# Batch 0's odd products ahead of the table scaling, and a third memset ahead of a sign change

## The chip, the cores and the metric

The kernel runs on one core of a Trainium2 chip. The metric is device time of one execution in microseconds (us); lower is better. A core has five engines that run side by side, each through its own list of instructions in order: PE (matrix products), ACT (activation and copies), DVE (vector arithmetic), POOL (a second vector engine, which also issues DMAs) and SP (which here only issues DMAs). They meet through semaphores: an instruction can be made to wait until another engine's counter has reached a value.

## The reference, cut to what matters

The input `x` is 8 sequences of 3136 positions by 256 features. The first block mixes it with a two-dimensional Fourier transform and keeps the real part; the second is a gated convolution with 1024 hidden features.

```python
X = np.fft.fft(x, axis=1)
X = np.fft.fft(X, axis=2)
x = X.real                               # (8, 3136, 256)

h = np.maximum(x @ w_in, 0.0)            # (8, 3136, 1024)
conv_out = sum over k of conv_w[k] * (h shifted by k - 1 along the sequence)
gate = 1.0 / (1.0 + np.exp(-conv_out))
out = h * gate @ w_out                   # (8, 3136, 256)
```

## The kernel before, in words

**The transform.** The kernel folds the sequence by its symmetries on DVE, multiplies the folded data with sine and cosine tables on PE, and combines the products on DVE into two tiles for each batch, `pt` and `qt`. The tables are `tab2` (even frequencies, `tabs[0]`) and `tab4` (odd ones, `tabs[1]`). Only half of each even table is loaded; `mirror_even(q)` (L269, ACT) writes the other half of fold class q from another class, with a sign. `mend_row(0, half)` (L310, ACT) multiplies the last rows of class 3 of `tab2`, for cosine and sine at once, with 1 or 0.5: it *halves the weight* of one row. It is one instruction on 2 partitions and 786 elements.

**Units.** The products of a batch come in units. A unit has products on PE (`part(0)` and `part(1)` issue the first two of them and the rest), a `copy` on ACT of one half of the PSUM result, and a `fin` on DVE. Of the four odd units of batch 0, `odds[0]` and `odds[2]` are `odd_even` units, which read `tab4`; `odds[1]` and `odds[3]` are `odd` units, whose part 1 is four products each that read class 2 of `tab2` and four weight tiles that `scaled()` (L217, ACT) has written into tiles named `h`. The copies are L394 and L417, the `fin` functions L398 to L430. After the odd units comes the *feature* unit, whose eight small products (into `pd`) read `tab2`, classes 3, 2, 1 and 0; then even units. In the profile these products are at L93, which is a helper that all products go through, so they are told apart by tile names.

**The waits.** The order on each engine is the order in which the code issues instructions. The waits are worked out from tiles: a read waits for the writes before it in code order, a write waits for the reads before it. `mend_row(0)` writes one instruction's worth of cosine and sine rows. Seen as one stretch of memory it runs from class 3 of the cosine table to class 3 of the sine table, and the sine table's class 2 lies inside. The products of `odds[1]` and `odds[3]` that read the sine table's class 2 therefore count as touching what `mend_row(0)` writes, though no element is shared.

**The steps.** After the transform of batch 0, the second block runs in *steps*, one for each batch, chunk of the sequence and slice of 128 hidden features. A step t has: `products` into `pb` and `pa` (PE), `copies` of `pb` into `nb` (L840, ACT), `combine` (L848, DVE, two instructions that add and clamp into the step's tile `h`), `seed` (L819, ACT), `first_tap` (L854, ACT), `middle` (L858, a DMA issued by POOL that adds `h` into `g`), `last_tap` (L863, DVE), `sigmoid` (L882, ACT), `gate` (L890, DVE) and `mm2` (the products into `po`, PE). `mm2` comes five cycles behind `products`. `row_of(step)` allots a step's tile `h` and, in a sequence's first chunk, has POOL zero its two edge columns (L825, a memset); `combine` waits for that.

**Around the first steps.** Up to about 104 us DVE also turns weights into f32 (`exponent` L651, `power` L655 on ACT, `sign` L661, `mantissa` L664, `lower` L667, `value` L670). `flip()` copies a row of `qt` by DMA into `er`; `store()` lets POOL change the sign of half of it (L490, the *sign change*), and SP then writes it out (L491).

The lines that the change moves on POOL are these, in the step loop's cycle t:

```python
        if 1 <= t < n - 1:
            row_of(steps[t + 1])
        if t < n:
            middle(steps[t])
        run("pool")          # cycle 0: store()
```

Of the kernel before, what the change touches and what calls it, by code (L numbers as in the profile page):

```python
# [37 lines left out]
def kernel(  # L38
# [226 lines left out]
    def mirror_even(q):  # L265

        for st, s in enumerate(((1.0, 1.0), (-1.0, 1.0), (-1.0, -1.0), (1.0, -1.0))[q]):
            of = st if q % 2 else 1 - st
            act(tabs[0][0:KR, st, q, HM:HE][:, ::-1], tabs[0][0:KR, of, q, 0:HE - HM], AF.Copy, scale=s)  # L269
# [37 lines left out]
    def mend_row(par, half):  # L307

        row = tabs[0][96:NP, 0:2, HQ - 1] if par == 0 else tabs[1][96:NP, 0:2, 1]
        act(row, row, AF.Copy, scale=half[96:NP])  # L310
# [401 lines left out]
    half = const.tile([P, 1], F32, name="half")  # L712
# [101 lines left out]
    def seed(s):  # L814

        b, c, f = s
        ch, n, fs = cut(s)
        pa[s] = psa.tile([P, 512], F32, name="pa", tag="pa")
        act(pa[s][:, 0:n], eb[b, c], AF.Copy, scale=ge[:, f:f + 1])  # L819

    def row_of(s):
        hs[s] = hp.tile([P, HW], F32, name="h", tag="h")
        w = chunks[s[1]].w
        if chunks[s[1]].zeros:
            nc.gpsimd.memset(hs[s][:, 0:w:w - 1], 0.0)  # L825

    def products(s):
        b, c, f = s
        ch, n, fs = cut(s)
        pb[s] = psb.tile([P, 512], F32, name="pb", tag="pb")  # L830
        mm(pb[s][:, 0:n], G[0:P - 1, 1, fs], PQ[b][1][0:P - 1, ch.k0:ch.k1], True, True)
        mm(pa[s][:, 0:n], G[:, 0, fs], PQ[b][0][:, ch.k0:ch.k1], False, True)

    def copies(s):

        ch, n, fs = cut(s)
        p = pb.pop(s)
        nb[s] = nbp.tile([P, 2, HN], F32, name="nb", tag="nb")
        for i, cols in enumerate((ch.fcols, ch.cols)):
            act(nb[s][:, i, cols], p[:, cols], AF.Copy, scale=-1.0 if i else 1.0)  # L840

    def combine(s):

        ch, n, fs = cut(s)
        a, c = pa.pop(s), nb.pop(s)
        h = hs[s]
        for i, (to, cols) in enumerate(((h[:, ch.front], ch.fcols), (h[:, ch.back][:, ::-1], ch.cols))):
            nc.vector._custom_dve(TENSOR_ADD_SAT, out=to, in0=a[:, cols], in1=c[:, i, cols],  # L848
                                  s0=BIG, s1=0.0)

    def first_tap(s):
        n = chunks[s[1]].w - 2
        gs[s] = gp.tile([P, HW - 2], F32, name="g", tag="g")[:, 0:n]
        act(gs[s], hs[s][:, 0:n], AF.Copy, scale=cw[:, 0, s[2]:s[2] + 1])  # L854

    def middle(s):
        n = gs[s].shape[1]
        nc.gpsimd.dma_start(out=gs[s], in_=hs[s][:, 1:1 + n], accum_op=ALU.add)  # L858

    def last_tap(s):  # L860
        g, h, f, k = gs[s], hs[s], s[2], 2
        n = g.shape[1]
        stt(out=g, in0=h[:, k:k + n], scalar=cw[:, k, f:f + 1], in1=g, op0=ALU.mult, op1=ALU.add)  # L863
# [14 lines left out]
    def sigmoid(s):  # L878

        v, p, r = shares(s)  # L880
        for c in [slice(0, r.stop)] if whole(s) else (slice(p.start, r.stop), v):
            act(gs[s][:, c], gs[s][:, c], AF.Sigmoid, scale=cw[:, 1, s[2]:s[2] + 1])  # L882

    def gate(s):

        b, c, f = s
        g, h = gs[s], hs.pop(s)[:, 1:]
        v, p, r = shares(s)
        if whole(s):
            vt(g, g, h[:, 0:r.stop], op=ALU.mult)  # L890
            return
        p = slice(p.start, r.stop)
        gt(g[:, p], g[:, p], h[:, p], op=ALU.mult)
        vt(g[:, v], g[:, v], h[:, v], op=ALU.mult)

    def keep(s):

        b, c, f = s
        r = shares(s)[2]
        if r.start < r.stop:  # L900
            nc.scalar.copy(out=left[:, f, b % 2 * LEFT:(b % 2 + 1) * LEFT], in_=gs[s][:, r])

    def mm2(s):
        b, c, f = s
        ch = chunks[c]
        tiles = [(gs[s][:, o:o + m], [(0, b, r, m)]) for o, r, m in ch.tiles]
        if ch.last and b % 2:
            tiles.append((left[:, f], [(i * LEFT, b - 1 + i, ch.rest[1], LEFT) for i in range(2)]))
        for i, (w, to) in enumerate(tiles):
            if f == 0 and i % 2 == 0:  # L910
                po[b, c, i // 2] = pso.tile([P, 2, D], F32, name="po", tag="po")
            pt = po[b, c, i // 2]
            mm(pt[:, i % 2, :], w, wout[:, f, :], f == 0 and i % 2 == 0, f == NF - 1)
            if f == NF - 1 and (i % 2 or i == len(tiles) - 1):
                del po[b, c, i // 2]
                osb = osp.tile([P, 2, D], F32, name="os", tag="os")
                for j in range(i - i % 2, i + 1):
                    nc.scalar.copy(out=osb[:, j % 2], in_=pt[:, j % 2])  # L918
                if i % 2:
                    r0, r1 = (tiles[j][1][0][2] for j in (i - 1, i))  # L920
                    nc.sync.dma_start(out=bass.AP(
                        tensor=out.tensor, offset=out.offset + (b * S + r0) * D,
                        ap=[[D, P], [(r1 - r0) * D, 2], [1, D]]), in_=osb)
                else:
                    for j, (p0, b_, r, m) in enumerate(tiles[i][1]):
                        (nc.scalar if j and s == steps[-1] else nc.sync).dma_start(out=rows[b_ * S + r:b_ * S + r + m, :], in_=osb[p0:p0 + m, 0])
        gs.pop(s)
# [11 lines left out]
    odds = [us[j] for j in (0, 1, 5, 6)]  # L939
# [28 lines left out]
        u.part(0)  # L968
    for u in odds[::2]:
        u.part(1)  # L970
    odds[0].copy()
    odds[0].fin()
    mend_row(0, half)
    odds[1].part(1)
    odds[1].copy()
    odds[1].fin()
    mirror_even(1)
    odds[2].copy()
    odds[2].fin()
    mirror_even(3)  # L980
    odds[3].part(1)
    odds[3].copy()
    odds[3].fin()
    exponent()
    mantissa()

    n = chunks[0].k1
# [14 lines left out]
            lower()  # L1002
    steps = [(b, c, f) for b in range(B) for c in range(len(chunks)) for f in range(NF)]
    per = len(chunks) * NF
    for i in range(2):
        row_of(steps[i])
    side = {}
    taken = set()
# [45 lines left out]
    for b in range(1, B):  # L1054
# [4 lines left out]
        n = per * b - (2 if b == 1 else 3) - c0  # L1059
# [12 lines left out]
    for b in range(1, B):  # L1072
        ops, singles, pres = fold_ops(b)
        c0, n = ends[b - 1], ends[b] - ends[b - 1]
# [4 lines left out]
        else:  # L1079
            if b == 2:  # L1080
                c0, n = c0 + 3, n - 3
# [16 lines left out]
    n = len(steps)  # L1098
# [6 lines left out]
    for t in range(n + LAG):  # L1105
        def run(where):
            for fn in side.get((t, where), []):
                fn()
        if 0 <= t - 4 < n:
            sigmoid(steps[t - 4])  # L1110
        if t + 1 < n:
            products(steps[t + 1])
            copies(steps[t + 1])
        run("first")
        run("act")
        if t >= LAG:
            keep(steps[t - LAG])
        if t < n:
            combine(steps[t])
        if t + 2 < n:  # L1120
            seed(steps[t + 2])
        if t < n:
            first_tap(steps[t])

        run("dve")
        if 0 <= t - 3 < n:
            last_tap(steps[t - 3])
        if 0 <= t - 4 < n:
            gate(steps[t - 4])
        if 1 <= t < n - 1:  # L1130
            row_of(steps[t + 1])
        if t < n:
            middle(steps[t])
        run("pool")
        run("load")
        if t >= LAG:
            mm2(steps[t - LAG])
        run("pe")
# [66 lines left out]
```

## Time and profile before

| what | value |
|---|---|
| device time, median of 3 runs | 1159.29 us (1159.04 to 1159.99) |
| the profiled execution: its time | 1159.72 us |
| the profiled execution: its span, first to last instruction | 1157.9 us |
| PE busy | 1137.4 us |
| DVE busy | 960.3 us |
| ACT busy | 901.4 us |
| POOL busy | 376.3 us |

Times in the profile are us from the start of the span; the mean duration of one instruction of a group is in ns. A row of the timeline is: start, duration, engine, line, operation, output tile <- input tiles, partitions x elements, count; in square brackets stands the engine's idle time before it and what ended that. Rows of like instructions that follow each other are merged. PE runs each f32 product as two records, so "x12" is six products. A letter q behind an engine's name is its queue, which issues DMAs.

### The profile page before, as it was taken

The numbers are of one execution on the slowest core, as the hardware profiler recorded it, in microseconds if no ns is written. First come the engines' busy times: TensorE is split into PE (matmuls) and PEld (weight loads), VectorE is DVE, ScalarE is ACT, GpSimd is POOL, SyncE is SP. The second block draws the span as 40 slices with busy tenths as digits, with TensorE's granted clock in tenths as the row PEclk, the third lists the DMA queues.
The fourth block names the chain that finished last, engine by engine and source line by source line (L and its number), as shares of the span: only waits on it lengthen the run. The fifth ranks groups of instructions, "written<-read, shape, count | busy, mean of one in ns | idle before, by whom it ended". The sixth has DMA issues, their size and how long they took to land.

```text
span 1157.9 us, 15068 instructions
## 1 busy us (share of the span) xinstructions
PE 1137.4 (98%) x4824; PEld 887.7 (77%) x4824; DVE 960.3 (83%) x1452; ACT 901.4 (78%) x1707; POOL 376.3 (32%) x484
## 2 busy tenths in 40 slices
PE   6999999999999999999999999999999999999998
PEld 4667787788777777778777777777778777777777
DVE  8899899988988989798878878888886767877775
ACT  3788868877787778787878778887877777888884
POOL 6425523642343242425132332422212222222223
PEclk9999999999999999999999999999999999999999
DMA  9787975876767586756676666765664656666664
GB/s 246 172 118 167 180 168 117 182 166 143 172 127 162 118 192 153 166 119 151 139 173 133 152 142 123 175 129 119 138 132 90 128 117 137 139 132 128 123 118 101
DMA packets 107595, 167.49 MB, mean 145 GB/s; under 512 B 32104, under 2 KB 62838, under 8 KB 107517
## 3 DMA queue, kind: packets, MB, share of 16 engines
q0 software_dynamic: 42160, 115.87, 51.9%
q1 hardware_dynamic: 64616, 50.53, 15.9%
q8 instruction: 38, 0.62, 0.2%
q10 hardware_dynamic: 741, 0.14, 0.1%
q14 instruction: 40, 0.33, 0.1%
HBM read 37.80 MB, written 25.74 MB: 55 GB/s over the span
## 4 chain that ended last, share of the span: by engine, by line
PE 85%; DVE 5%; ACT 5%; issue 2%; POOL 2%; DMA 1%; SPq 0%; ACTq 0%; POOLq 0%; DVEq 0%
PE po L93 53%; PE pb L93 13%; PE pa L93 13%; PE pd L93 6%; DVE g L863 1%; DVE g L890 1%; ACT os L918 1%; ACT nb L840 1%; POOL xh L129 1%; DMA xh<-in_x_dram 1%; DVE h L848 1%; ACT pa L819 1%; ACT g L882 0%; ACT g L854 0%; DMA tab<-dft_seq_dram 0%
## 5 line engine op out<-in xcount | busy, mean ns | idle before, releaser
L93 PE MATMUL po<-wout,g 128*128 128x256 f32 x3072 | 706.4, 379 | 3.8 <-DVE g L890 3.7
L93 PEld LDWEIGHTS po<-wout,g 128*128 128x128 f32 x3072 | 580.5, 190 | 149.0 <-DVE g L890 18.2
L858 POOL DMA_DIRECT2D g<-h x256 | 220.0, 859 | 729.3 <-ACT g L854 459.9
L840 ACT ACTIVATE nb<-pb 128x386 f32<-128x386 f32 (+3 forms) x512 | 227.5, 499 | 168.0 <-PE pb L93 167.1
L848 DVE CUSTOM_DVE_ANT_0 h<-pa,nb 128x386 f32<-128x386 f32 (+3 forms) x512 | 265.2, 559 | 34.8 <-PE pa L93 22.6
L882 ACT ACTIVATE g<-g,cw 128x770 f32<-128x770 f32 (+3 forms) x264 | 246.0, 935 | 46.3 <-DVE g L863 44.9
L863 DVE SCALAR_TENSOR_TENSOR g<-h,cw,g 128x770 f32<-128x770 f32 (+1 forms) x256 | 265.6, 1038 | 0.3 <-DMA g<-h 0.3
L890 DVE TENSOR_TENSOR g<-g,h 128x770 f32<-128x770 f32 (+1 forms) x248 | 240.3, 969 | 22.3 <-ACT g L882 22.1
L854 ACT ACTIVATE g<-h,cw 128x770 f32<-128x770 f32 (+1 forms) x256 | 244.1, 953 | 0.0
L93 PE MATMUL pb<-qt,G 127*128 127x387 f32 (+2 forms) x512 | 213.7, 498 | 1.5 <-ACT nb L840 1.1
L93 PE MATMUL pa<-pt,G 128*128 128x387 f32 (+2 forms) x512 | 212.1, 495 | 0.8 <-ACT pa L819 0.7
L819 ACT ACTIVATE pa<-eb,ge 128x387 f32<-128x387 f32 (+2 forms) x256 | 155.3, 607 | 2.1 <-DVE h L848 0.3
L93 PEld LDWEIGHTS pa<-pt,G 128*128 128x128 f32 x512 | 96.6, 189 | 75.6 <-issue 18.5
L129 POOL DMA_INDIRECT xh<-in_x_dram,idx x64 | 98.4, 1538 | 20.2 <-issue 12.7
L93 PE MATMUL pd<-tab,w 98*128 98x197 f32 (+2 forms) x448 | 97.6, 317 | 0.0
L93 PEld LDWEIGHTS pb<-qt,G 127*128 127x128 f32 x512 | 90.9, 190 | 8.5 <-ACT nb L840 2.9
L93 PEld LDWEIGHTS pd<-tab,w 98*128 98x128 f32 (+1 forms) x448 | 82.0, 191 | 8.9
L918 ACT COPY os<-po 128x256 f32<-128x256 f32 x196 | 57.4, 393 | 6.3 <-PE po L93 6.3
L398 DVE TENSOR_TENSOR as<-as,pd 128x196 f32<-128x196 f32 x14 | 5.0, 358 | 46.0 <-ACT as L394 46.0
L176 POOL COPY w<-xh 98x4 f32<-98x4 f32 (+1 forms) x30 | 37.5, 1251 | 7.9 <-DVE xh L170 7.9
L154 DVE TENSOR_TENSOR xh<-xh 98x1020 f32<-98x1020 f32 (+1 forms) x32 | 38.7, 1211 | 0.5 <-DMA xh<-in_x_dram,idx 0.5
L165 DVE TENSOR_TENSOR xh<-xh 98x1024 f32<-98x1024 f32 (+1 forms) x32 | 38.9, 1216 | 0.1
(150 smaller groups left out, 430.9 us busy)
## 6 DMA issues: line engine op xcount, KB each, us to landing
g<-h POOLq DMA_DIRECT2D x192, 385.0 KB, 3.9
g<-h POOLq DMA_DIRECT2D x64, 416.0 KB, 4.3
out_dram<-os SPq DMA_DIRECT2D x96, 256.0 KB
xh<-in_x_dram SPq DMA_DIRECT2D x16, 784.0 KB
eb<-ed SPq DMA_DIRECT2D x16, 193.5 KB
raw<-in_moe_w_in_dram SPq DMA_DIRECT2D x4, 512.0 KB
raw<-in_moe_w_out_dram SPq DMA_DIRECT2D x1, 2048.0 KB
eb<-ed SPq DMA_DIRECT2D x8, 209.0 KB
```

The source lines that it names most:

```text
L93: nc.tensor.matmul(o, l, r, start=start, stop=stop, skip_group_check=True)
L129: nc.gpsimd.indirect_dma_start(out=xh[b, h][0:NP, 7 - m].rearrange("p q d -> p (q d)"), out_offset=None, in_=bass.AP(tensor=x.tensor, offs ...
L165: vt(flat(to, to + 2), flat(0, 2), flat(2, 4), op=op)
L819: act(pa[s][:, 0:n], eb[b, c], AF.Copy, scale=ge[:, f:f + 1])
L840: act(nb[s][:, i, cols], p[:, cols], AF.Copy, scale=-1.0 if i else 1.0)
L848: nc.vector._custom_dve(TENSOR_ADD_SAT, out=to, in0=a[:, cols], in1=c[:, i, cols], s0=BIG, s1=0.0)
L854: act(gs[s], hs[s][:, 0:n], AF.Copy, scale=cw[:, 0, s[2]:s[2] + 1])
L858: nc.gpsimd.dma_start(out=gs[s], in_=hs[s][:, 1:1 + n], accum_op=ALU.add)
L863: stt(out=g, in0=h[:, k:k + n], scalar=cw[:, k, f:f + 1], in1=g, op0=ALU.mult, op1=ALU.add)
L882: act(gs[s][:, c], gs[s][:, c], AF.Sigmoid, scale=cw[:, 1, s[2]:s[2] + 1])
L890: vt(g, g, h[:, 0:r.stop], op=ALU.mult)
L918: nc.scalar.copy(out=osb[:, j % 2], in_=pt[:, j % 2])
```

## The change

The change has two parts, both in how the code is written in order; no instruction is added or taken away.

1. Batch 0's odd units: `odds[1].part(1)` and `odds[3].part(1)` stand ahead of all copies, of `mend_row(0, half)` and of the last two mirrored tables, `mirror_even(1)` and `mirror_even(3)`. Before, `odds[1].part(1)` stood behind `mend_row`, and `odds[3].part(1)` behind both mirrors.
2. `row_of` is called for three steps, not two, ahead of the step loop; the loop's own calls begin one cycle later.

```diff
     for u in odds[::2]:
         u.part(1)
-    odds[0].copy()
-    odds[0].fin()
-    mend_row(0, half)
-    odds[1].part(1)
-    odds[1].copy()
-    odds[1].fin()
-    mirror_even(1)
-    odds[2].copy()
-    odds[2].fin()
-    mirror_even(3)
-    odds[3].part(1)
-    odds[3].copy()
-    odds[3].fin()
+    for u in odds[1::2]:
+        u.part(1)
+    for u, f in zip(odds, (lambda: mend_row(0, half), lambda: mirror_even(1), lambda: mirror_even(3), lambda: None)):
+        u.copy()
+        u.fin()
+        f()
     exponent()
     mantissa()
...
-    for i in range(2):
+    for i in range(3):
         row_of(steps[i])
...
-        if 1 <= t < n - 1:
+        if 2 <= t < n - 1:
             row_of(steps[t + 1])
```

The order of instructions on PE, ACT and DVE is the same before and after; the first part changes only who waits for whom. Below, - is before and + is after; the names in brackets are the counters that a row waits for (`Activation_49` is ACT's, `DMASW` and `DMAHW` are DMA queues), `tab_109` is `tab2`, and the rows of `po<-tab_109,h` are the eight products of part 1 of `odds[1]` and `odds[3]`.

On PE, from the last `odd_even` products to the feature unit:

```order
 L93 MATMUL po<-tab_110,w 128x196 [waits Activation_49]
 L93 MATMUL po<-tab_110,w 128x196 x2
-L93 MATMUL po<-tab_109,h 128x197 [waits Activation_49] x3
-L93 MATMUL po<-tab_109,h 128x197 x5
+L93 MATMUL po<-tab_109,h 128x197 [waits Activation_49] x4
+L93 MATMUL po<-tab_109,h 128x197 x4
 L93 MATMUL pd<-tab_109,ea 1x197 [waits DMASW4_49,Activation_49,Pool_49]
 L93 MATMUL pd<-tab_109,ea 1x196
```

Before, the third of the eight products waits for `mend_row(0)`; after, the first four wait for the four weight tiles of L217, one each, and none for `mend_row(0)`.

On ACT, the same place, from the weight tiles (L217) to the copies of the feature unit (L450):

```order
 L217 ACTIVATE h<-w,turn 98x256 x2
 L394 COPY as<-po 128x196 [waits PE_49]
-L310 ACTIVATE tab_109<-tab_109,half 2x2x393
-L417 COPY as<-po 128x197 [waits PE_49]
+L310 ACTIVATE tab_109<-tab_109,half 2x2x393 [waits PE_49]
+L417 COPY as<-po 128x197
 L269 ACTIVATE tab_109<-tab_109 99x196 x2
 L394 COPY as<-po 128x196 [waits DVE_49,Activation_49]
 L269 ACTIVATE tab_109<-tab_109 99x196 [waits Activation_49]
 L269 ACTIVATE tab_109<-tab_109 99x196
-L417 COPY as<-po 128x197 [waits DVE_49,PE_49]
+L417 COPY as<-po 128x197 [waits DVE_49]
```

`mend_row(0)` (L310) now waits for PE. In the built program the count it waits for is that of the last of the eight products; the copies behind it, which before waited for PE themselves, are covered by that wait.

On POOL, around the sign change (L490) and the DMAs of steps 0 and 1 (L858):

```order
 L458 TENSOR_TENSOR er<-h 1x196 [waits Activation_49]
 L459 TENSOR_TENSOR er<-h 1x196
-L825 MEMSET h 128x2 x2
+L825 MEMSET h 128x2 x3
 L858 DMA g<-h 128x770 [waits DMASW1_49,DVE_49,Activation_49]
 L490 TENSOR_SCALAR er<-er 1x392 [waits DMAHW1_49]
-L825 MEMSET h 128x2
 L858 DMA g<-h 128x770 [waits DMASW2_49,DVE_49,Activation_49]
 L825 MEMSET h 128x2 [waits PE_49]
```

The memset of step 2's tile moves from behind step 0's DMA and the sign change to ahead of both. The last row is step 3's memset, which keeps its place.

## The prediction

> **What bounds the kernel now.** I read the page first, then PE's waits, then the busy time by stretches, and last the timeline of the two places that the change touches.
>
> The page: the span, and the busy time of each engine.
>
> ```profile
> span 1157.9 us, 15068 instructions
> PE 1137.4 (98%) x4824; PEld 887.7 (77%) x4824; DVE 960.3 (83%) x1452; ACT 901.4 (78%) x1707; POOL 376.3 (32%) x484
> ```
>
> PE is idle for 1157.9 - 1137.4 = 20.5 us in all, so no change of waits can bring more than that. PE's waits over the whole run (engine, tile, line <- releaser: us in total, times, longest) show how little of it this change can reach:
>
> ```profile
> PE po L93 <- DVE g L890: 3.7, 8, 1.1
> PE po L93 <- ACT tab L310: 0.9, 1, 0.9
> ```
>
> The second row is the wait that part 1 of the change takes away. The next rows give the busy time in stretches (length, then PE, PEld, DVE, ACT and POOL busy with counts, the granted clock, DMA share, GB/s); the last row is DVE's only wait of over 0.15 us in 49.75 to 104 (the one that ends at 49.70, on the boundary).
>
> ```profile
> 49.70:81.20 31.50, 28.86 (x112) 19.69 (x110) 31.22 (x52) 26.65 (x49) 10.00 (x21) 1.00 0.87 138
> 81.20:104.00 22.80, 22.08 (x90) 16.11 (x91) 22.30 (x33) 20.14 (x55) 12.00 (x10) 1.00 0.78 177
> 104.00:137.00 33.00, 33.00 (x141) 25.47 (x141) 30.08 (x44) 27.17 (x51) 18.53 (x17) 1.00 0.82 166
> ...
> DVE h L848 <- POOL h L825: 2.2, 1, 2.2
> ```
>
> From 49.7 to 104 DVE has no room (31.22 of 31.50, 22.30 of 22.80), while PE idles; behind 104 PE is busy all the time (33.00 of 33.00). So the first 104 us decide: whatever moves DVE's work at about 50 moves PE at about 104, and from there the shift stays to the end.
>
> **Place 1: the eight products and the table scaling.** PE, ACT and DVE between 27 and 33 us:
>
> ```profile
> 27.60 0.86 PE L93 MATMUL po<-tab,h 98*128 98x197 f32 x4
> 29.33 2.37 PE L93 MATMUL po<-tab,h 98*128 98x197 f32 x12 [0.87 <-ACT tab L310]
> 31.88 0.88 PE L93 MATMUL pd<-tab,ea 99*1 99x197 f32 x16 [0.18 <-issue]
> ...
> 28.01 0.30 ACT L394 COPY as<-po 128x196 f32<-128x196 f32 x1
> 28.33 0.94 ACT L310 ACTIVATE tab<-tab,half 2x786 f32<-2x786 f32 x1
> 30.34 0.33 ACT L417 COPY as<-po 128x197 f32<-128x197 f32 x1 [1.06 <-PE po L93]
> 30.68 0.62 ACT L269 ACTIVATE tab<-tab 99x196 f32<-99x196 f32 x2
> 31.21 0.30 ACT L394 COPY as<-po 128x196 f32<-128x196 f32 x1
> 31.42 0.62 ACT L269 ACTIVATE tab<-tab 99x196 f32<-99x196 f32 x2
> ...
> 30.69 0.36 DVE L423 TENSOR_TENSOR as<-as,po 128x196 f32<-128x196 f32 x1 [1.00 <-ACT as L417]
> ```
>
> The reader should see a zigzag. PE does two of the eight products, waits 0.87 us for ACT's scaling (28.33 to 29.27), does six; ACT then waits 1.06 us for the first of those units. Part 1 removes PE's wait: 31.70, where the six end now, becomes 31.70 - 0.87 = 30.83, or some 0.15 earlier, since the third product then streams right behind the second. I take 30.7. That is a gain of 1.0 us on PE.
>
> But the wait has changed sides. The scaling (L310) was free at 28.33; it now waits for the last of the eight products, so it starts at 30.7, not 28.33. Behind it in ACT's list stand the copy L417, the mirror L269, the copy L394, the mirror L269, the copy L417, and then the feature unit's copies. L417 starts 0.94 less a pipeline overlap of up to 0.09 (30.68 + 0.62 against 31.21) behind 30.7: at 31.55 to 31.64 instead of 30.34. That is 1.2 to 1.3 later; the new wait costs ACT more than the 1.06 us idle that it replaces. DVE's L423 waits for this copy and moves as far. PE's next work, the feature products at 31.88, needs the first mirrored half of the last L269 pair (31.42 + 0.31 = 31.73, then 31.88). It moves to 33.1. So PE idles from 30.7 to 33.1, 2.4 us, where it idled 0.87 + 0.18. PE gained 1.0 and then lost it and 1.2 more. I take **+1.2 us** for everything behind; bounds are 0 (should the scaling not be late) and +1.4.
>
> PE's timeline from 31.88 to 45 has no idle of 0.15, and what follows waits for PE or for what follows PE, so the 1.2 is carried on PE, ACT, DVE and POOL to about 47 us. Loads that already run are not moved, and none of those waits is theirs.
>
> **Place 2: the third memset.** DVE, POOL and PE between 46 and 53 us:
>
> ```profile
> 46.81 0.71 DVE L667 SCALAR_TENSOR_TENSOR raw<-raw,left 128x512 f32<-128x512 uint32 x1
> 49.70 1.02 DVE L848 CUSTOM_DVE_ANT_0 h<-pa,nb 128x385 f32<-128x385 f32 x2 [2.19 <-POOL h L825]
> 50.65 0.68 DVE L661 SCALAR_TENSOR_TENSOR win<-raw,win 128x512 int32<-128x512 int32 x1
> 51.36 0.69 DVE L670 SCALAR_TENSOR_TENSOR win<-raw,win 128x512 f32<-128x512 f32 x1
> 51.97 0.42 DVE L651 TENSOR_SCALAR wout<-raw 128x512 int32<-128x512 int32 x1
> 52.31 1.02 DVE L848 CUSTOM_DVE_ANT_0 h<-pa,nb 128x385 f32<-128x385 f32 x2
> ...
> 46.97 0.99 POOL L858 DMA_DIRECT2D g<-h  x1 [8.84 <-ACT g L854]
> 47.67 1.98 POOL L490 TENSOR_SCALAR er<-er 1x392 f32<-1x392 f32 x1
> 49.52 0.14 POOL L825 MEMSET h<- 128x2 f32 x1
> 49.66 0.90 POOL L858 DMA_DIRECT2D g<-h  x1
> 50.27 0.40 POOL L825 MEMSET h<- 128x2 f32 x1
> ...
> 50.04 0.81 PE L93 MATMUL pa<-pt,G 128*128 128x386 f32 x2
> ```
>
> DVE's combine of step 2 (49.70) waits 2.19 us for a memset of 0.14 us, which stands on POOL behind step 0's DMA and the sign change of 1.98 us. After the change the memset runs while POOL is idle (8.84 us idle before 46.97), so it costs nothing, and no DMA is moved by its length. Combine 2 then starts when DVE is free: 47.51 before, so 47.51 + 1.2 = 48.7, which is 1.0 ahead of 49.70.
>
> What of this 1.0 reaches combine 3, at 52.31? First, its input: `pa` of step 3 ends on PE at 50.04 + 0.81 = 50.85, now 52.05. Combine 3 can't start ahead of about 52.1, so at most 0.2 of the 1.0 is left. Second, what DVE does in between (L661, L670, L651, 1.66 us from L661's start to combine 3) now runs beside the sign change. Step 0's DMA moves to 48.17 and the sign change to 48.87, until 50.85. L661 starts 0.95 behind combine 2, at 49.65, in the middle of it. Rows at the end of the run show what such a pair does: a DVE instruction with two SBUF inputs beside a POOL instruction that reads SBUF, and the same one alone.
>
> ```profile
> 1122.56 1.28 POOL L893 TENSOR_TENSOR g<-g,h 128x448 f32<-128x448 f32 x1
> ...
> 1122.80 1.47 DVE L894 TENSOR_TENSOR g<-g,h 128x384 f32<-128x384 f32 x1 [0.54 <-ACT g L882]
> ...
> 1139.11 0.55 DVE L894 TENSOR_TENSOR g<-g,h 128x384 f32<-128x384 f32 x1
> ```
>
> The DVE instruction takes 1.47 us instead of 0.55 and ends 0.43 behind POOL's end (1123.84): it stood still until POOL was done. L661 reads `raw` and `win`, both in SBUF. By this row it ends 0.68 - 0.12 = 0.56 behind 50.85, at 51.41; L670 starts 0.03 later, L651 0.61 behind that, combine 3 another 0.34 later: 52.4, against 52.31. That is **+0.1**. Without the standstill it would be 52.1, or -0.2. Both bounds stay in the range; I take +0.1, since the rows with two SBUF inputs are the nearest. Step 1's DMA (now 50.86) and step 3's memset (51.5 to 51.9) come in time for that.
>
> [...]
>
> **The sum.** +1.2 from place 1, at most -1.0 from place 2, of which -0.2 net is left at combine 3 and +0.1 with the standstill. DVE carries +0.1 through its full stretch to 104, PE takes it there. The profiled execution took 1159.72 (span 1157.9), 0.43 above the median; a shift applies to both, so 1159.29 + 0.1 = **1159.4**. Alone, part 1 would give +1.2, and part 2 would let combine 3 start at about 51.2, -1.1.
>
> **Rivals.**
> B: the scaling is not late, because its wait ends earlier than I read it or ACT makes it up. For it: L417 waits for PE now too, and no trace shows the new wait. Against: the count is that of the last product. Then +1.2 falls away and -1.1 (place 2 alone) to -1.4 (the whole 50.85 for `pa`) is left: 1157.9 to 1158.2.
>
> C, on the slower side: PE's 2.4 us of idle time lowers its clock. The start of the run shows what a slow clock costs.
>
> ```profile
> 9.39 3.78 PE L93 MATMUL pa<-win 128*128 128x512 f32 x4 [3.79 <-issue]
> 12.96 1.91 PE L93 MATMUL pb<-win 128*128 128x512 f32 x2
> 15.66 4.46 PE L93 MATMUL pb<-win 128*128 128x512 f32 x10
> ```
>
> Behind 3.79 us of idle time a record of 128x512 takes about 0.9 us; from 15.66 on 0.45. The six slow records reach from 9.39 to about 14.7 (each starts a little ahead of the other's end), 5.3 us. As long a one from 33.1 would do half its work, and lose 2.6 us; `pa` of step 3 would end at 52.05 + 2.6 = 54.7, and combine 3 would start 2.4 later than now: 1161.7. Against it: the stretches above show a granted clock of 1.00, with waits of up to 1.1 us in them. It decides from the point where 2.4 us of idle are enough.
>
> [...]
>
> D: L661 gets at its operands ahead of the sign change, which then waits for L661 and L670, until 51.0. It needs 47.96 (the end of step 0's DMA) to 49.65, 1.7 us, so it ends at 52.7; step 1's DMA and step 3's memset follow 1.0 later (49.66 to 50.27, plus 0.40), and combine 3 waits until 53.7: +1.4, 1160.7. Against it: the sign change starts 0.8 ahead of L661.
>
> **How the numbers follow.** A measurement of this kernel can tell about 0.2%, or 2.3 us, from no change. Forecast A 0.70, B 0.08, C 0.10, D 0.12. A's own range is 1158.8 (-0.2, and 0.3 for runs, whose three times lie 0.95 apart) to 1160.2. A and D hold 0.82, 1158.8 to 1160.7; for the spread of runs, and towards B and C, I give 1158.2 to 1161.3. A, B and D lie within 0.2%: 0.90, of which I leave 0.04 to a gain that grows in DVE's full stretch and 0.02 to a loss there. With C that makes faster 0.04, same 0.84, slower 0.12.
>
> **What would show it.** Right: PE's wait for L310 is gone, and before `pd` stands one of about 2.4 us for L269; ACT's L310 starts at about 30.7; DVE's wait for POOL's L825 is gone; L661 at about 49.7 takes some 1.8 us; combine 3 starts at about 52.4; PE's waits behind 104 are as they were. Wrong: L310 still starts at 28.3 (B), products of this size, six in 2.37 us, take twice that behind 33 us (C), the sign change takes over 3 us and combine 3 waits for L825 (D), or PE idles differently behind 104, which nothing here foresees.

## The result, and the profile after

The changed kernel is slower, and it no longer has one time: seven runs gave 1160.22, 1162.09, 1162.28, 1166.65, 1166.68, 1166.79 and 1166.81 us (median 1166.65), where seven runs of the kernel before lie between 1159.04 and 1159.99 (median 1159.67). The ratio is 1.0042, with an interval of 1.0022 to 1.0063. The forecast was 1159.4, in a range up to 1161.3.

The mean granted clock of PE tells the runs apart. It was 0.999 or 1.000 in every run of the kernel before for which it is on record; here it was 0.998 in the run of 1160.22, 0.997 in the two of 1162, and 0.993 in the four of 1166.7. The profiled execution is one of these: 1166.65 us, span 1164.9 us.

The stretch from 25 to 66 us of it (length; PE, PEld, DVE, ACT and POOL busy with counts; granted clock; DMA share; GB/s), cut at the two changes of the clock, 32.24 and 49.31, with two stretches of 3.41 us ahead of the first:

```profile
25.41:28.83 3.42, 3.42 (x22) 3.42 (x21) 3.35 (x5) 2.47 (x9) 1.11 (x2) 1.00 1.01 386
28.83:32.24 3.41, 1.78 (x11) 1.46 (x9) 0.95 (x4) 1.54 (x4) 2.19 (x3) 1.00 1.05 395
32.24:49.31 17.07, 16.15 (x66) 13.35 (x67) 10.51 (x25) 6.28 (x18) 4.61 (x10) 0.50 0.51 105
49.31:66.37 17.06, 15.55 (x71) 11.04 (x70) 15.48 (x28) 15.00 (x33) 5.64 (x8) 1.00 0.50 109
```

At 32.24 the clock falls to half, and it stays there for 17.07 us. The kernel before has a granted clock of 1.00 from 14.94 us, where the clock's first record in its trace begins, to the end of its span.

PE around that place, in the timeline of the changed kernel:

```profile
27.65 2.96 PE L93 MATMUL po<-tab,h 98*128 98x197 f32 x16
33.16 1.49 PE L93 MATMUL pd<-tab,ea 99*1 99x197 f32 x16 [2.55 <-issue]
34.58 2.03 PE L93 MATMUL po<-tab,w 99*128 99x99 f32 x8
...
41.57 4.59 PE L93 MATMUL po<-tab,w 99*128 99x99 f32 x16
45.96 1.49 PE L93 MATMUL pb<-qt,G 127*128 127x386 f32 x2
```

The eight odd products (16 records) run in one go, as forecast, from 27.65 to 30.61. Then PE stands still for 2.55 us. The feature products start at 33.16, against 31.88 before: 1.28 later. From there to the first product of the steps (`pb`) it takes 12.80 us (33.16 to 45.96); before, 7.07 (31.88 to 38.95). That is 5.7 us of loss in work that has not changed. A group like `99x99 x8` takes 2.03 us instead of 1.14.

ACT in the same place:

```profile
27.59 0.30 ACT L394 COPY as<-po 128x196 f32<-128x196 f32 x1
30.65 0.94 ACT L310 ACTIVATE tab<-tab,half 2x786 f32<-2x786 f32 x1 [2.77 <-PE po L93]
31.62 0.32 ACT L417 COPY as<-po 128x197 f32<-128x197 f32 x1
...
32.70 0.62 ACT L269 ACTIVATE tab<-tab 99x196 f32<-99x196 f32 x2
```

The scaling (L310) waits 2.77 us for PE and starts at 30.65; the copy behind it is at 31.62 (30.34 before). The forecast had 30.7, 31.6 and, for the feature products, 33.1. The profile names no releaser for PE's 2.55 us ("issue"), but the last pair of mirrors (L269), which these products read, starts at 32.70; half of the pair (0.31) and another 0.15 later, as before the change, is 33.16.

DVE and POOL around step 2's combine and step 3's, in the same kernel:

```profile
55.27 1.02 DVE L848 CUSTOM_DVE_ANT_0 h<-pa,nb 128x385 f32<-128x385 f32 x2 [0.23 <-ACT nb L840]
56.21 1.01 DVE L661 SCALAR_TENSOR_TENSOR win<-raw,win 128x512 int32<-128x512 int32 x1
59.13 1.02 DVE L848 CUSTOM_DVE_ANT_0 h<-pa,nb 128x385 f32<-128x385 f32 x2 [0.85 <-PE pa L93]
...
55.78 1.99 POOL L490 TENSOR_SCALAR er<-er 1x392 f32<-1x392 f32 x1
```

The 2.19 us wait for the memset is gone. Step 3's combine now waits for `pa`, which everything ahead of it made late: 59.13 against 52.31. The last product of the run starts 6.92 later than before (1159.96 against 1153.04), so the 6.8 us lost by 59 us reach the end whole.

### The profile page after: what moved, and what is told of

The parts are those of the page before. It is cut to its first block, busy times and chain, and to the rows that moved or that the text cites. A ratio compares the mean times of both kernels' runs of the same rounds, so it can differ in the third digit from the quotient of the medians.

```text
span 1164.9 us, 15069 instructions
## 1 busy us (share of the span) xinstructions
PE 1143.3 (98%) x4824; PEld 893.9 (77%) x4824; DVE 961.3 (83%) x1452; ACT 901.3 (77%) x1707; POOL 376.8 (32%) x484
## 4 chain that ended last, share of the span: by engine, by line
PE 86%; DVE 5%; ACT 4%; issue 2%; POOL 2%; DMA 0%; ACTq 0%; POOLq 0%; DVEq 0%
PE po L93 53%; PE pb L93 14%; PE pa L93 13%; PE pd L93 6%; DVE g L863 1%; DVE g L890 1%; ACT os L918 1%; DVE h L848 1%; ACT nb L840 1%; POOL xh L129 1%; POOL w L176 1%; ACT g L882 0%; ACT pa L819 0%; DMA raw<-in_moe_w_in_dram 0%; ACT g L854 0%
## 5 line engine op out<-in xcount | busy, mean ns | idle before, releaser
L858 POOL DMA_DIRECT2D g<-h x256 | 219.9, 859 | 734.8 <-ACT g L854 465.6
```

## The experiments

Two theories were set against each other. T1: PE's idle stretch of 2.55 us lets the clock fall to half, and that is the whole loss. T2: the loss comes with something else in the change, the third memset and what it lets collide, and the clock only goes along with it.

### Part 1 alone

The kernel before, with `odds[1].part(1)` and `odds[3].part(1)` ahead of the copies, as in the first part of the diff; two memsets as before.

> Part 1 alone (the products ahead of the scaling; two memsets as before). Theory T1 (PE's idle stretch of 2.5 us ahead of the feature products lets the granted clock drop to half, and that is the whole loss): the stretch is here too, so the mean clock is below 0.999 in most runs, and the time lies between 1160.5 (the 1.2 us of the later scaling) and 1168, slower than before. Rival T2 (the loss comes with the third memset: the sign change beside DVE's work, or what DVE's earlier work collides with): no loss beyond 1.2 us, about 1160.9, clock 1.000.

Measured: five runs between 1162.12 and 1167.95, median 1163.19 (ratio 1.0043, 1.0026 to 1.0060), with mean clocks of 0.999, 0.996 (three times) and 0.992. One more execution took 4273.72 us at full clock and is left out as disturbed; nothing here explains it. Stretches of the profiled run:

```profile
30.10:33.51 3.41, 0.86 (x18) 0.39 (x17) 2.01 (x6) 2.92 (x8) 2.80 (x3) 1.00 1.06 362
33.51:40.33 6.82, 6.82 (x32) 6.82 (x29) 4.72 (x12) 1.61 (x6) 4.19 (x8) 0.50 1.02 184
```

The idle stretch (30.11 to 32.66) is there, and from 33.51, 0.85 us behind its end, the clock is at half, here for 6.82 us. So the loss comes with part 1, and T2 as written falls.

### Part 2 alone

```diff
-    for i in range(2):
+    for i in range(3):
         row_of(steps[i])
...
-        if 1 <= t < n - 1:
+        if 2 <= t < n - 1:
             row_of(steps[t + 1])
```

> Part 2 alone (three memsets; the products as before). T1: no new idle stretch on PE, so clock 1.000; DVE's 2.19 us wait for the memset goes and combine of step 3 starts about 1.1 us earlier: 1158.2 to 1158.8. T2: slower than before, by up to 7 us, with or without a lower clock.

Measured: 1158.07 (1157.56 to 1158.75 in ten runs), beside 1159.08 of the kernel before in the same job (1158.75 to 1159.72); the ratio is 0.9992, 0.9982 to 1.0001, an interval that just includes no change. The clock was 0.999 or 1.000 in all. The gain is 1.0 us, as the forecast's working had it (1.1); the median lies a little below the range expected here. DVE in its profile:

```profile
46.91 1.02 DVE L848 CUSTOM_DVE_ANT_0 h<-pa,nb 128x385 f32<-128x385 f32 x2
47.85 0.79 DVE L661 SCALAR_TENSOR_TENSOR win<-raw,win 128x512 int32<-128x512 int32 x1
...
50.52 1.03 DVE L848 CUSTOM_DVE_ANT_0 h<-pa,nb 128x385 f32<-128x385 f32 x2 [0.82 <-PE pa L93]
```

Combine 2 no longer waits; combine 3 waits 0.82 us for `pa`, which is where most of the rest of the 2.19 us went.

### The idle stretch filled

The changed kernel, with idle products in the stretch. `keep_on` is the kernel's own helper; its products' result is read by nobody.

```diff
     for u in odds[1::2]:
         u.part(1)
+    keep_on(3)
```

> The changed kernel with three idle products of 128x512 on PE (0.85 us each at full clock, 2.55 us in all) between the eight odd products and the feature products; their result is read by nobody. T1: PE has no idle stretch, the clock stays at 1.000, and the time is that of the forecast, 1159.2 to 1160.0, the same as before. T2: the fill changes nothing that matters: 1162 to 1167.

Measured: 1159.04 (1158.88 to 1160.00 in ten runs), ratio 0.9999 (0.9990 to 1.0009), clock 0.999 or 1.000 in all; the median lies 0.16 us below the range expected with T1. PE's timeline has no gap there:

```profile
27.26 2.97 PE L93 MATMUL po<-tab,h 98*128 98x197 f32 x16
30.06 2.74 PE L93 MATMUL pb<-win 128*128 128x512 f32 x6
32.78 0.88 PE L93 MATMUL pd<-tab,ea 99*1 99x197 f32 x16
```

ACT's scaling still waits for PE, the feature products still start late, the third memset is still there: all of the change is in place, and 2.7 us of useless work on PE make it as fast as the kernel before. This is the run that settles it for T1.

### Less fill

`keep_on(1)` and `keep_on(2)` in the same place.

> The changed kernel with one idle product of 128x512 in the stretch (0.85 us), so that some 1.7 us of PE's idle time are left. T1 with a threshold near 2.5 us: clock 1.000 and 1159 to 1160. T1 with a lower threshold (the changed kernel's clock fell when only 1.6 us of the stretch were over): a clock below 0.999 in some or all runs, and 1160.5 to 1168 in those.

> The changed kernel with two idle products of 128x512 in the stretch, so that some 0.85 us of idle time are left, as long as the one that the kernel before has for the scaling. T1 by any threshold above 0.9 us: clock 1.000, 1158.9 to 1159.6.

With one product, 1.69 us of idle time are left: 1160.12, from 1159.19 to 1162.15 in ten runs, ratio 1.0007 (0.9998 to 1.0017). Five of the runs have a mean clock of 0.997 or 0.998 and lie at 1160.65 and above; the other five have 0.999 or 1.000 and lie between 1159.19 and 1159.59. The profiled run is one of the first five:

```profile
31.19:34.60 3.41, 2.00 (x26) 1.53 (x27) 3.12 (x9) 2.17 (x8) 2.58 (x3) 1.00 1.07 312
34.60:38.02 3.42, 3.42 (x14) 3.42 (x13) 2.33 (x7) 1.29 (x5) 3.28 (x8) 0.50 0.96 214
```

So 1.7 us of idle time were enough in five of ten runs. With two products 0.83 us are left: 1159.08 (1158.91 to 1159.75), clock 1.000 in all ten runs. The profiled run's stretch that holds the whole gap, and one of the kernel before that holds all but 0.13 us of its gap of 0.87:

```profile
29.94:33.35 3.41, 2.58 (x22) 0.80 (x20) 1.98 (x6) 2.89 (x8) 2.79 (x3) 1.00 1.06 366
```

```profile
28.59:32.01 3.42, 2.50 (x16) 2.19 (x20) 2.38 (x7) 2.33 (x7) 2.20 (x4) 1.00 1.04 396
```

### The idle time alone, in the kernel before

Three idle copies on ACT ahead of the scaling; order, waits and memsets as before. PE's old wait for the scaling grows from 0.87 to 2.70 us.

```diff
+    for _ in range(3):
+        act(left[:, 0:4].rearrange("p f i -> p (f i)"), con, AF.Copy)
     mend_row(0, half)
     odds[1].part(1)
```

> The kernel before (order, waits and two memsets unchanged) with three idle ACT copies of 128x512 ahead of the scaling, some 0.6 us each; nothing reads them. PE's wait for the scaling grows from 0.87 to some 2.7 us, and all that follows moves by 1.85 us. T1 (idle time is the cause wherever it comes from): the clock falls below 0.999 in most runs, and the time lies between 1162 and 1169. If part 1's order or its waits are needed for the loss: clock 1.000 and 1160.9 to 1161.3.

Measured: 1167.65 (1162.07 to 1169.54 in six runs), ratio 1.0059 (1.0039 to 1.0078); clocks 0.999, 0.996, 0.993, 0.992 and twice 0.991. Two runs lie a little above the expected 1169.

```profile
27.03:30.44 3.41, 1.00 (x6) 0.68 (x5) 2.49 (x6) 3.33 (x7) 1.76 (x3) 1.00 1.04 393
30.44:50.92 20.48, 20.19 (x77) 17.01 (x78) 10.33 (x25) 7.11 (x20) 5.79 (x10) 0.50 0.46 117
```

Without any of the change the clock falls, for 20.48 us, behind 3.41 us in which PE was idle for 2.41. Idle time is the cause in this kernel too.

### Wide products behind the stretch

What was open is why the clock stays low for so long: PE is busy for 16.15 of the 17.07 us. The start of the run suggests that the kind of work matters: in the kernel before the first seven records of 128x512, from 9.39 us, start 0.85 to 1.01 us apart, those from 15.23 on 0.43, and the trace's first record of the clock, at 1.00, begins between the two, at 14.94. That the wide products bring the clock up is the author's estimate from these numbers; no run shows it. The changed kernel, with five idle products of 128x512 behind the feature products:

```diff
         u.matmuls(0, 1)
+        if i == 0:
+            keep_on(5)
```

> The changed kernel with five idle products of 128x512 right behind the feature products (their result is read by nobody; 4.3 us at full clock, 8.5 at half). The idle stretch of 2.5 us stays, so the clock falls as in the changed kernel; the question is how long it stays low. D1 (a stretch of wide products, like those at the start of the run, brings the clock back at the next window's edge or the one after): low for at most 2 or 3 windows of 3.41 us in every run, mean clock 0.995 or more. D2 (the length does not depend on what PE does): mean clock down to 0.992 or 0.993 in about half of the runs, as in the changed kernel.

Measured: 1164.90 (1163.99 to 1166.83 in four runs), ratio 1.0050 (1.0033 to 1.0066), with mean clocks of 0.997, 0.998, 0.999 and 1.000. The low stretches profiled so far are 5, 2, 1 and 6 times 3.41 us long; the windows of D1 are such steps. One of them at half clock takes 0.0015 off the mean (half of 3.41 in some 1163 us), so by this estimate none of the four runs has more than two, and the run at 1.000 has none: there the clock did not fall, though the program is the same. In the profiled run it is one:

```profile
30.40:33.82 3.42, 1.35 (x18) 0.65 (x19) 2.50 (x8) 2.82 (x10) 2.81 (x3) 1.00 1.06 351
33.82:37.24 3.42, 3.42 (x6) 1.36 (x5) 2.37 (x5) 0.94 (x3) 3.09 (x6) 0.50 1.01 234
37.24:47.48 10.24, 10.14 (x55) 7.76 (x54) 4.61 (x11) 3.50 (x8) 0.59 (x4) 1.00 0.36 53
```

That is as D1 expects, but four runs are few where the changed kernel itself had, by the mean clock, one run of seven with one step and two with two. It makes D1 likely; it doesn't show it. As a remedy it is worthless: even the run at a clock of 1.000 took 1163.99 us, 4.8 more than the kernel before beside it.

### Neither engine waits

The false touch between the scaling and the odd products comes from one instruction that spans cosine and sine. Here it is two:

```diff
-        row = tabs[0][96:NP, 0:2, HQ - 1] if par == 0 else tabs[1][96:NP, 0:2, 1]
-        act(row, row, AF.Copy, scale=half[96:NP])
+        if par == 0:
+            for st in range(2):
+                row = tabs[0][96:NP, st, HQ - 1]
+                act(row, row, AF.Copy, scale=half[96:NP])
+            return
+        row = tabs[1][96:NP, 0:2, 1]
+        act(row, row, AF.Copy, scale=half[96:NP])
```

First in the changed kernel, with the third memset; then alone, in the kernel before.

> The changed kernel with the scaling of the even table's rows written as two instructions, one for cosine and one for sine, so that it and the odd products no longer count as touching each other and neither waits. T1: ACT's scaling starts at 28.3, the first odd copy at about 29.4 (30.3 before), the feature products at about 30.9 (31.9 before) with less than 0.4 us idle ahead of them; clock 1.000; combine of step 3 about 2.1 to 2.4 us earlier than before: 1157.0 to 1157.6, faster than before. T2: the loss stays, 1162 to 1167.

> The kernel before with nothing but the scaling written as two instructions (cosine, sine); order and two memsets as before. The odd products and the scaling no longer touch: PE's wait of 0.87 us goes and nothing waits in its place, the feature products start about 1.0 us earlier, clock 1.000: 1158.0 to 1158.5, between the kernel before and the changed kernel with the split (1157.2).

In the changed kernel: 1157.23 (1156.96 to 1157.66 in ten runs), ratio 0.9984 (0.9974 to 0.9994), clock 0.999 or 1.000. None of the runs overlaps with the kernel before: this version beats both. PE and ACT in its timeline (five lines were added above, so the scaling is L312 and the first odd copy L422):

```profile
27.57 2.96 PE L93 MATMUL po<-tab,h 98*128 98x197 f32 x16
30.72 0.88 PE L93 MATMUL pd<-tab,ea 99*1 99x197 f32 x16 [0.19 <-issue]
...
27.77 1.13 ACT L312 ACTIVATE tab<-tab,half 2x393 f32<-2x393 f32 x2
29.18 0.33 ACT L422 COPY as<-po 128x197 f32<-128x197 f32 x1 [0.27 <-PE po L93]
```

The scaling runs while PE works, 1.13 us for the two against 0.94 for one, and PE's idle time ahead of the feature products is 0.19 us. Alone the split gives 1158.60 (1158.47 to 1159.21 in ten runs) against 1159.17 of the kernel before beside it, ratio 0.9995 (0.9985 to 1.0004): 0.6 us, not clear of the noise and 0.1 short of the expected range. The gain in the changed kernel was 1.85 us, and its time lies inside the expected range; the gain is mostly the memset's 1.0 and the split's 0.6.

## Why the prediction was wrong

**Place 1 was right in its mechanism and its size.** The wait changed sides as described. The scaling started at 30.65 (30.7), the feature products at 33.16 (33.1), after 2.55 us of idle time (2.4). With the stretch filled, where nothing else differs, the price can be read from two runs: filled 1159.04 less part 2 alone 1158.07, 0.97 us for the forecast's 1.2.

**Place 2 was right but for one term.** Combine 3 is bound by `pa`, as the first limit there had it. The standstill of L661 beside the sign change was given as 1.1 us and measured 0.33 in the changed kernel, 0.11 with part 2 alone and 0.09 with the fill. So combine 3 waited for `pa` in all three: the case behind the forecast's bound of -0.2 came, not the one behind +0.1.

**The sum holds where the clock does.** The fill run is the change without the fall of the clock: 0.04 us under the kernel before beside it, against +0.1 forecast. That the two are so near is partly luck, since the +0.1 rests on the standstill that did not come.

**What failed is rival C, in its chance and its price.** It had 0.10, because nothing in the trace before showed an idle stretch between 1.1 and 3.8 us. The clock fell in all seven runs, and the sum that gave 1159.4 has no term for it. The step that failed is "against it: the stretches above show a granted clock of 1.00, with waits of up to 1.1 us in them": that is true of 1.1 us and says nothing of 2.4. The neighbouring row, the only one with longer idle time, was the start, which spoke for C. The price was taken from the start as well: 5.3 us with records of twice the time, read as half clock (the trace has no record of the clock ahead of 14.94 us), 2.6 lost. In the profiled run it was 17.07 us, and by the first product of the steps 5.7 us were lost. Over the whole run the fall cost the profiled execution some 7 us: it took 6.98 us more than the median of the kernel before, where the fill run, without the fall, took 0.04 us less. `pa` of step 3 came 8.1 us late (58.15 against 50.04), but combine 3 only 6.8, because it had not been bound by `pa` before, and the end 6.9.

**How the clock fell was not in the trace before.** In five profiled runs it was low for 17.07, 6.82, 3.42, 20.48 and 3.42 us, which are 5, 2, 1, 6 and 1 times 3.41. In the 3.41 us ahead of the fall PE was idle for a part only: it was busy for 1.78 us of them in the changed kernel, 0.86 with part 1 alone, 2.00 with one product of fill, 1.00 in the idle-time run and 1.35 of 3.42 in the last one.

**The range and the chances.** The range ended at 1161.3, and one run of seven lies in it. Slower by over 2.3 us had a chance of 0.12; it is what came.

## What to carry to other kernels

A wait that is taken off one engine by moving code must be followed to the engine that now waits, and PE's idle time there must be compared with the longest that the trace has seen at full clock, not only added to the sum. Here gaps of up to 1.1 us were free (1.10 ahead of 81.21 in the kernel before, clock 1.00), and one of 1.7 us was not always (five of ten runs). Where two instructions touch only because one of them spans a stretch that neither shares, cutting that instruction in two takes the wait off both sides; moving code only chooses who waits (here 0.87 us on PE and 1.06 on ACT before, 2.55 and 2.77 with the code moved, 0.19 and 0.27 with the split).

## What the runs showed of the hardware that was not expected

- In the five profiled runs in which the clock fell, the 3.41 us ahead of the fall had PE busy for 0.86, 1.00, 1.35, 1.78 and 2.00 us. It did not fall behind stretches as long at that place with 2.50, 2.55 and 2.58 (the kernel before, part 2 alone, two products of fill), nor behind later ones of the kernel before with 2.31 (79.79 to 83.20) and 2.32. The rows of part 2 alone and of a later stretch of the kernel before, with the one behind it, are these:

```profile
26.33:29.75 3.42, 2.55 (x15) 2.23 (x14) 3.18 (x7) 2.41 (x6) 1.30 (x2) 1.00 1.05 402
...
55.90:59.31 3.41, 2.32 (x7) 0.81 (x5) 3.38 (x6) 3.41 (x6) 0.85 (x3) 1.00 1.10 254
59.31:62.72 3.41, 3.29 (x14) 2.77 (x15) 3.38 (x8) 2.88 (x6) 0.89 (x3) 1.00 1.25 134
```

- PE's busy time in such a stretch is not all that decides. The last products of the changed kernel (128x256) leave one with 1.93 us, less than the 2.00 above, and the clock stays at 1.00 behind it to the end of the span. What else counts is open.

```profile
1158.63:1162.04 3.41, 1.93 (x9) 1.34 (x8) 0.00 (x0) 2.02 (x7) 0.00 (x0) 1.00 0.54 181
1162.04:1164.88 2.84, 0.00 (x0) 0.00 (x0) 0.00 (x0) 0.00 (x0) 0.00 (x0) 1.00 0.35 106
```

- The clock's records in the traces have lengths in steps of 3.413 us: 335 steps from 14.94 us on in the kernel before; 5 at full, 5 at half and 327 at full clock from 15.17 on in the changed kernel. The stretches of these two kernels above are counted in these steps. The fall is not tied to the end of the gap: it came 0.92 us ahead of it in the changed kernel (32.24 against 33.16), 0.85 behind it with part 1 alone (33.51 against 32.66) and 1.35 behind it with the wide products (33.82 against 32.47). That the place of the steps parts the runs with 1.69 us of idle time into five and five is the author's estimate; no run shows it.
- Once low, the clock stays low for 1 to 6 of these steps though PE's records are busy nearly all the time (6.82 of 6.82 us with part 1 alone, 16.15 of 17.07 in the changed kernel). What ends it is open; wide products behind the gap went with at most two steps in four runs, by their mean clocks. In the changed kernel the clock came back, at 49.31, behind the step that holds the first products of 386 columns (`pb`, at 45.96); in the idle-time run the low stretch reaches past them too (77 records of PE, of which 72 lie ahead of `pb`). With part 1 alone and with one product of fill it came back without them (low stretches of 32 and 14 records), so width alone does not explain it.
- The sign change on POOL has a record of 2.0 us, but L661, a DVE instruction with two SBUF inputs that began beside it, was held up only until 0.76 to 0.80 us behind the record's start (56.21 + 0.33 against 55.78, for one), and the next one, L670, took its 0.69 us while the record ran on (57.26 against 57.77, in the changed kernel). In the rows that the forecast took its standstill from, the DVE instruction ended 0.43 us behind the POOL record. So the length of POOL's record is not the time for which L661 was held up; what held it up is open, and no run here tests a cause.
